# Attention and MLP-mixer on one Trainium2 core: output sums by accumulating DMAs, GpSimd's sums on VectorE, weight sums staged in four places

## The chip, the core and the metric

The kernel runs on one NeuronCore of a Trainium2 chip. TensorE multiplies matrices into PSUM; VectorE, ScalarE and GpSimd do elementwise work; DMAs move data between DRAM and SBUF and are issued from the instruction queues of SyncE (SP), ScalarE or GpSimd. Each engine works its own queue in order. The metric is the device time of one execution in microseconds (us), given as the median of several runs.

## What is computed

```python
kv  = einsum('bhsd,bhse->bhde', k, v)          # 8 batches, 8 heads, 576 tokens, head size 64
out = einsum('bhsd,bhde->bhse', q, kv)
x   = (out / sqrt(mean(out*out, -1) + 1e-6) * g_norm)  # (B,H,S,D) -> x of (B, S, H*D) = (8, 576, 512)
h   = relu(x.transpose(0,2,1) @ w_tok1) @ w_tok2       # token mixing, 576 -> 256 -> 576
u   = x + h.transpose(0,2,1)
out = u + relu(u @ w_ch1) @ w_ch2                      # channel mixing, 512 -> 1536 -> 512
```

All data are 32-bit floats on the chip.

## The kernel before

**First part (to about 197 us).** Attention and token mixing of the eight batches give `u`. Each batch's first 512 tokens are a *unit* in DRAM (`u_dram[0..7]`); the ninth unit holds the last 64 tokens of all batches. Unit 0 is group 0; units 2g-1 and 2g are group g, so groups 1 to 4 have 1024 tokens each.

**Channel mixing by fast multiplication.** Each of the two products with `w_ch1` and `w_ch2` is done by a 2x2 block scheme with seven products instead of eight (Winograd's form of Strassen's), for groups 1 to 4 at two levels: 7 outer times 7 inner products. The scheme needs sums of blocks on every side: sums of the weights, sums of `u` or of the middle result `v`, and sums of the products.

- *Group 0* uses one level: `channel1_once(0)` (TensorE from about 197 us) and `channel2_once(0)` (from 234 us). Beside them run, woven in by `weave`, the sums of the weights for the inner level (`split`): for each weight and outer product o, four sums of 128x384 in a staging tile `sv0`, then DMAs of the seven parts to DRAM (`parts_dram`). In `split`, `first` also sends three unchanged parts; `first` and `second` add on VectorE, `third` and `fourth` on GpSimd; `fourth` issues the DMAs of the four sums. For weight 1 the staging pool has two buffers, for weight 2 one (`svb`, L1292). All these DMAs are issued on SP. `channel2_once` runs its products in the order first, sixth, second, seventh, fifth, fourth, third; product `fourth` adds into the PSUM tile that `seventh` filled, after VectorE has read it there (`u3`, L781), and `third` likewise into that of `fifth`.
- *Groups 1 to 4* run `channel1(g)` and `channel2(g)`. Time is counted in *places*: one inner product is one place, 49 places a stage, and the dictionaries `products` and `beside` say which product and which other steps stand at a place. The program order of every engine is the order of places, kept by `keep_in_program_order`. Channel1 of group g begins at place 98(g-1), its channel2 49 places later, and the next group's channel1 follows without a break. A `put(b + place, ...)` in channel2 with a place above 48 therefore lies in the next group's channel1, and a negative place lies in the stage before.

**One outer product** (`outer`, L816). Its seven inner products use three PSUM names: `a` and `b` with one buffer, `d` with two. Product 1 fills `a`, ScalarE copies it to `d`; product 5 fills `b` and is read as `p5`; product 6 adds into `d`, which is read as `u2`; then products 2, 3, 7 and 4, at the places 0, 1, 3, 4, 5, 6 and 9 of the outer product (`PLACE`, L809). Between a product and the next one that needs its bank back there are at least two places, in which the eviction has to be done. VectorE does the two joins of each outer product, and all six evictions where a base is added (in channel1 for o = 2, 5, 4); otherwise ScalarE copies.

**Other steps in the places.** `inner_u` and `outer_u`: sums of blocks of `u` for the inner and outer level. `inner` (`ins`): sums of `v` for the inner level of channel2, tile `sv`. `add`, `sum1` to `sum4`, `make_a21`: outer sums of `v`. `rectify`: relu by ScalarE. In channel1, outer sum 1 of `v` (four 128x768) and outer sum 7 (two 128x1536) are on GpSimd (L955, L957). `turn_blocks`: VectorE transposes of the next group's units (one `xt` buffer, fetched from `u_dram` by `fetch_t`), whose blocks go to DRAM and come back as `uT` by `fetch_u`. `fetch_w`: the weight parts from `parts_dram`, asked for 4 to 12 places before the first place of their outer product, with two buffers each.

**The output.** An outer product of channel2 leaves a tile [128, 4, 256] in the pools `us` or `r` (three buffers each). `us` also holds the outer sums 5, 6 and 4 of `u`. `xg` holds the group's `u` (fetched by `fetch_x`); nine `xadd` steps of 128x1024 on VectorE add the tiles onto it, one `radd` adds product 6 to product 7, and `store` writes `xg` to the output. Seven of the nine stand at places 45 to 60 of channel2.

Of the kernel before, what the change touches and what calls it, by code (L numbers as in the profile page):

```python
# [20 lines left out]
def kernel(  # L21
# [255 lines left out]

    def split(weight, o):

        at = []  # L280
        wide = lambda t: t if weight == 1 else t.rearrange("p (w e) -> p w e", w=W)
        to = parts_dram[weight, o]

        def of(n):
            if weight == 1:
                return (w_ch1[:, SA[o]] if SA[o] < 4 else late["w2"][:, SA[o] - 4])[:, SA[n]]
            return w2_of(o)[:, ts(int(n in (2, 3)), W), ts(int(n in (7, 3)), P)]

        own = lambda n: wide(at[0][:, OWN[weight][n]])

        def first():
            at.append(late["sv0"].tile([P, 4, FQ], F32, name="sv0"))
            for n in (1, 2, 4 if weight == 1 else 3):
                dma(wide(to[:, POS[n]]), of(n))
            if weight == 1:
                tensor_add(own(5), of(7), of(4))
            else:
                tensor_add(own(5), of(7), of(1), ALU.subtract)

        def second():  # L300
            tensor_add(own(6), own(5), of(1), ALU.subtract) if weight == 1 else tensor_add(
                own(6), of(3), own(5), ALU.subtract)

        def third():
            tensor_add(own(7), of(1 if weight == 1 else 3), of(7), ALU.subtract, nc.gpsimd)

        def fourth():
            tensor_add(own(3 if weight == 1 else 4), of(2), own(6), ALU.subtract, nc.gpsimd)
            t = at[0]
            if weight == 1:  # L310
                dma(to[:, 1:].rearrange("p (g k) f -> p g k f", k=3)[:, :, :2],
                    t.rearrange("p (g k) f -> p g k f", k=2))
            else:
                dma(to[:, 1:3], t[:, :2])
                dma(to[:, 5:], t[:, 2:])

        return [first, second, third, fourth]


# [598 lines left out]
    def channel1(g, n0):  # L918
# [19 lines left out]
        for i, o in enumerate(ORDER1):  # L938
            first(i, o)
            for place, step in zip((-4, -2, 2, 5), inner_u(g, o)):  # L940
# [11 lines left out]
        for place, step in zip((15, 18), add(3, 3, 1)):  # L952
            put(b + place, step)
        for place, i, j in ((27, 0, 0), (29, 0, 1), (30, 1, 1), (32, 1, 0)):
            put(b + place, do(lambda i, j: tensor_add(*(sub(v_tile(g, t), i, j) for t in (1, 4, 3)),  # L955
                                                      engine=nc.gpsimd), i, j))
        for place, step in zip((36, 39), add(7, 5, 4, nc.gpsimd)):  # L957
            put(b + place, step)

        for t, *places in ((2, None, 24, 28, 26), (7, 46, 46, 48, 48), (1, None, 44, 47, 45)):  # L960
# [4 lines left out]
        for k, place in enumerate((12, 17, 23, 27, 33, 37, 42, 46)):  # L965
# [4 lines left out]
        put(b + 70, do(fetch_t, units(g + 2)[0], 0))  # L970
        for place, step in zip((-2, 1, 10, 18), outer_u(g)):
# [3 lines left out]
    def channel2(g, n0):  # L975
# [86 lines left out]
        for place, steps in (  # L1062
                (-12, [ins[1][0]]), (-11, [ins[1][2]]), (-10, [ins[1][1]]), (-8, [ins[1][3]]),
                (3, [ins[2][0]]), (5, [ins[2][1]]), (6, [ins[4][0]]), (7, [ins[2][2]]),
                (8, [A[0]]), (9, [A[1]]), (10, [ins[2][3]]), (11, [S3[0]]), (12, [S3[1]]),
                (13, [ins[4][1]]), (14, [ins[4][2]]), (15, [S2[0]]), (16, [ins[4][3]]), (17, [ins[7][0]]), (18, [xadd(0, 0, 1)]),
                (19, [ins[7][1]]), (21, [S2[1], ins[7][2]]), (23, [ins[7][3]]), (24, [S1[0]]),
                (25, [ins[6][0]]), (26, [S4[0]]), (27, [ins[6][1]]), (28, [S1[1]]), (29, [ins[6][2]]),
                (31, [ins[5][0], ins[6][3]]), (33, [ins[5][1]]), (34, [xadd(0, 0, 2)]),
# [4 lines left out]
        if g < NG - 1:  # L1074
            for place, steps in ((45, [xadd(0, 1, 6)]), (48, [radd(7, 6)]), (50, [xadd(1, 0, 4)]),
                                 (52, [xadd(1, 1, 5)]), (54, [xadd(1, 0, 7)]), (56, [xadd(1, 1, 7)]),
                                 (56, [do(store, g, 1)]), (58, [xadd(0, 1, 5)]),
                                 (60, [xadd(0, 1, 3)]), (60, [do(store, g, 0)]),
                                 (74, [do(fetch_x, g + 1, 0)]), (84, [do(fetch_x, g + 1, 1)])):
                put(b + place, *steps)  # L1080
# [8 lines left out]
        for k in range(4):  # L1089
            put(b + 6 + 2 * k, do(fetch_u, g + 1, k // 2, k % 2))  # L1090
# [201 lines left out]
    late["sv0"] = pool("svb", 1, "right", w2s)  # L1292
    fill, turns = lasts + parts2[:20], turn_unit(2)
    for i, f in enumerate(turns):
        fill.insert(3 * i, f)
    fill.insert(1, do(fetch_u, 1, 0, 0))
    fill.insert(4, do(fetch_u, 1, 0, 1))
    for k in range(4):
        fill.insert(8 + 4 * k, do(fetch_w, 0, k))
    fill.insert(24, do(fetch_w, 1, 0))  # L1300
    fill += [do(fetch_u, 1, 1, 0), do(fetch_u, 1, 1, 1), do(fetch_w, 1, 1)] + inner_u(1, 1)[:2] + outer_u(1)[:1]
    weave(channel2_once(0), fill)
# [12 lines left out]
    for n, f in enumerate(parts2[20:]):  # L1315
        put(2 + 3 * n // 2, f)
    put(2, do(fetch_t, units(2)[0], 0))
    put(16, turn_over)
    put(22, do(fetch_x, 1, 0))
    put(26, do(fetch_x, 1, 1))  # L1320
# [43 lines left out]
```

## Time and profile before

| | |
|---|---|
| median of 7 runs | 869.25 us (867.01 to 871.2) |
| the profiled execution | 870.09 us |
| its span, first to last instruction | 868.3 us |
| mean granted TensorE clock | 0.975 of full speed |
| PE busy | 795.6 us (92%) |
| DVE busy | 641.8 us (74%) |
| ACT busy | 265.1 us (31%) |
| POOL busy | 118.4 us (14%) |
| moved by DMA | 197.36 MB |

Engines are named as in the profile: PE is TensorE's matmul, PEld its weight load, DVE VectorE, ACT ScalarE, POOL GpSimd, SP SyncE (SPq and POOLq are the queues on which DMAs are issued). A line of a timeline gives start and duration in us, the engine, the line of the kernel, the operation, the tile written and the tiles read, partitions x elements, how often it is merged, and in brackets the idle time before it with what ended it. Since helpers record most operations, L122 stands for every elementwise sum and L131 for every matmul: the names of the tiles tell them apart. A line of waits gives the total in us, the number of times and the longest. A line of DMA issues gives the number, the KB of each, and the median us from issue to landing.

### The profile page before, as it was taken

To read this page: it belongs to the slowest core of one execution; us is meant where nothing else is said; L and a number is where in the kernel's file an instruction comes from. 1 tells how busy PE (TensorE), PEld (TensorE's weight loads), DVE (VectorE), ACT (ScalarE), POOL (GpSimd) and SP (SyncE) were. 2 spreads that over 40 slices of the span, in tenths; PEclk is the share of its full clock that TensorE was granted. 3 is DMA by queue.
4 is the path that set the end of the run, shared out by engine and by line. 5 is a ranking of instruction groups with operands and counts; after the bars stand their busy time and mean duration, and the time that the engine had idled before them with its cause. 6 is when DMAs were issued, how large, how long until landed. Compare 5 with 4: busy or idle time off the path is not lost.

```text
span 868.3 us, 14846 instructions
## 1 busy us (share of the span) xinstructions
PE 795.6 (92%) x5832; PEld 658.5 (76%) x5832; DVE 641.8 (74%) x890; ACT 265.1 (31%) x513; POOL 118.4 (14%) x97
## 2 busy tenths in 40 slices
PE   6999999999995698899998799999889999979995
PEld 5655545448884576799987699997779998769995
DVE  3667575986744497878688969778887868895985
ACT  2366565741100122421143052123242113305210
POOL 1302010102413205100002400000510000240000
PEclk9999999999998799999999999999999999999997
DMA  9999993666999987685467867448678546655542
GB/s 296 312 336 340 344 381 131 220 195 208 352 289 298 314 271 241 182 264 157 136 232 239 252 210 233 132 143 292 210 238 276 141 143 221 216 157 140 144 134 73
DMA packets 124773, 197.36 MB, mean 227 GB/s; under 512 B 9376, under 2 KB 75424, under 8 KB 124704
## 3 DMA queue, kind: packets, MB, share of 16 engines
q1 hardware_dynamic: 120400, 185.24, 68.3%
q0 software_dynamic: 2624, 9.44, 2.8%
q10 hardware_dynamic: 1680, 1.74, 0.7%
q8 instruction: 46, 0.75, 0.4%
q14 instruction: 23, 0.19, 0.1%
HBM read 148.80 MB, written 47.58 MB: 226 GB/s over the span
## 4 chain that ended last, share of the span: by engine, by line
PE 50%; DVE 15%; DMA 7%; issue 2%; SPq 2%; POOL 1%; ACT 0%; DVEq 0%; POOLq 0%; ACTq 0%
PE ps_d L131 22%; PE ps_b L131 14%; PE ps_a L131 13%; DVE v L122 4%; DVE sv L122 4%; DMA xt<-u_dram 3%; SPq L119 2%; DVE ui L122 2%; DMA parts<-sv 2%; DVE y L590 1%; DVE u L122 1%; DVE xg L122 1%; POOL sv L122 1%; PE ps_u L131 1%; DMA w<-parts 1%
## 5 line engine op out<-in xcount | busy, mean ns | idle before, releaser
L131 PE MATMUL ps_d<-ui,w 128*128 128x256 f32 x504 | 127.4, 399 | 26.4 <-DVE v L122 13.3
L131 PEld LDWEIGHTS ps_d<-ui,w 128*128 128x128 f32 x504 | 98.0, 199 | 46.9 <-DVE v L122 18.4
L122 POOL TENSOR_TENSOR v<-v,v 128x768 f32<-128x768 f32 (+1 forms) x24 | 57.7, 2409 | 410.6 <-ACT v L128 376.8
L128 ACT COPY ps_d<-ps_a 128x768 f32<-128x768 f32 (+1 forms) x56 | 32.0, 571 | 223.0 <-PE ps_a L131 223.0
L131 PE MATMUL ps_b<-w,sv 128*128 128x128 f32 x672 | 84.9, 276 | 3.9 <-DVE sv L122 3.9
L131 PE MATMUL ps_a<-w,v 128*128 128x128 f32 x672 | 84.2, 275 | 0.0
L131 PEld LDWEIGHTS ps_b<-w,sv 128*128 128x128 f32 x672 | 79.5, 192 | 4.8 <-DVE sv L122 4.7
L131 PEld LDWEIGHTS ps_a<-w,v 128*128 128x128 f32 x672 | 79.8, 192 | 0.2
L122 DVE TENSOR_TENSOR v<-v,v 128x1536 f32<-128x1536 f32 (+1 forms) x46 | 74.4, 1624 | 0.3
L125 ACT ACTIVATE v<-v 128x768 f32<-128x768 f32 (+1 forms) x54 | 42.6, 821 | 95.7 <-DVE v L122 93.4
L131 PE MATMUL ps_d<-w,v 128*128 128x128 f32 x528 | 67.0, 277 | 2.7 <-DVE xg L122 2.7
L131 PE MATMUL ps_u<-h,w_tok 128*128 128x512 f32 (+1 forms) x160 | 67.5, 607 | 0.4 <-ACT ps_u L128 0.2
L131 PEld LDWEIGHTS ps_d<-w,v 128*128 128x128 f32 x528 | 63.4, 194 | 3.0 <-DVE xg L122 2.9
L131 PE MATMUL ps_h<-x,w_tok 128*128 128x512 f32 (+1 forms) x160 | 65.5, 603 | 0.1
L131 PE MATMUL ps_d<-w,sv 128*128 128x128 f32 x480 | 60.1, 275 | 0.0
L131 PE MATMUL ps_b<-ui,w 128*128 128x256 f32 x168 | 42.8, 392 | 18.3 <-DVE ui L122 12.1
L131 PEld LDWEIGHTS ps_d<-w,sv 128*128 128x128 f32 x480 | 57.1, 192 | 0.2
L131 PEld LDWEIGHTS ps_b<-ui,w 128*128 128x128 f32 x168 | 32.3, 195 | 25.2 <-DVE ui L122 12.5
L131 PE MATMUL ps_a<-uT,w 128*128 128x256 f32 x192 | 50.1, 400 | 0.7 <-DVE v L122 0.5
L131 PEld LDWEIGHTS ps_h<-x,w_tok 128*128 128x128 f32 (+1 forms) x160 | 26.1, 189 | 32.1 <-issue 27.7
L131 PEld LDWEIGHTS ps_u<-h,w_tok 128*128 128x128 f32 (+1 forms) x160 | 24.7, 179 | 31.5 <-issue 25.4
L122 DVE TENSOR_TENSOR sv<-v 128x768 f32<-128x768 f32 x40 | 48.6, 1222 | 0.0
(141 smaller groups left out, 1250.9 us busy)
## 6 DMA issues: line engine op xcount, KB each, us to landing
w<-parts SPq DMA_DIRECT2D x168, 384.0 KB, 3.6
w<-parts SPq DMA_DIRECT2D x56, 192.0 KB, 3.1
qT<-in_q_dram SPq DMA_DIRECT2D x8, 1152.0 KB, 9.3
xt<-u_dram SPq DMA_DIRECT2D x36, 256.0 KB, 4.3
blocks<-y SPq DMA_DIRECT2D x72, 128.0 KB, 2.5
uT<-blocks SPq DMA_DIRECT2D x36, 256.0 KB, 4.7
xg<-u_dram SPq DMA_DIRECT2D x9, 1024.0 KB, 6.4
k_in<-in_k_dram SPq DMA_DIRECT2D x16, 512.0 KB, 9.3
```

The costliest lines, as they stand in the source:

```text
L119: keep(engine.dma_start(o, i))
L122: keep(engine.tensor_tensor(out=o, in0=a, in1=b, op=op))
L125: keep(nc.scalar.activation(o, a, AF.Relu))
L128: keep(nc.scalar.copy(o, a))
L131: keep(nc.tensor.matmul(*a, **kw))
L590: keep(nc.vector.transpose(blocks[u][:, :, o, n:n + 2].rearrange("p b n t -> p n b t"), xt[u, i][:, ts(o, DH)].rearrange("p (n b t) -> p n ...
```

## The change

- In `split`, weight 2's staging is no longer one buffer: four places are used in turn, in halves of the tiles v3 and v2 of group 1. All its sums are on VectorE, its DMAs are issued on ScalarE's queue, and the DMAs of a staged split are issued when the next split's fourth sum has been issued. Weight 1 is as before.
- The fill of `channel2_once(0)` is written out anew: all 28 steps of weight 2's sums, the transposes of unit 2, the loads of `uT`, the four inner sums and two outer sums of `u` for group 1 lie in it. Before, eight of the steps and the rest of the `u` sums lay beside channel1 of group 1. `turn_over` moves from place 16 to 9.
- In channel1, GpSimd's six sums go to VectorE, at other places; `inner_u`, `outer_u` and `rectify` get other places; of the eight `turn_blocks`, four lie in channel1 and four in channel2 (places 49 to 80).
- In channel2, the sums of the first outer product stand at -3 to 2 and no longer at -12 to -8; S4 moves from 26 to 29. For groups 1 to 3 `xg` is not fetched: two DMAs copy `u` from DRAM to the output, and nine DMAs on GpSimd's queue add the tiles onto it (`accum_op=ALU.add`); `radd` stays. Group 4 keeps `xg` and `xadd`.

```diff
+        queue, other = (nc.sync, nc.gpsimd) if weight == 1 else (nc.scalar, nc.vector)
...
         def first():
-            at.append(late["sv0"].tile([P, 4, FQ], F32, name="sv0"))
+            if weight == 1:
+                at.append(late["sv0"].tile([P, 4, FQ], F32, name="sv0"))
+            else:
+                n = len(staged)
+                flat = v_tile(1, 3 - n // 2 % 2).rearrange("p s j t -> p (s j t)")
+                at.append(flat[:, ts(n % 2, 4 * FQ)].rearrange("p (k f) -> p k f", k=4))
...
+        def fourth():
+            tensor_add(own(3 if weight == 1 else 4), of(2), own(6), ALU.subtract, other)
+            if weight == 1:
+                put_away()
+            else:
+                staged.append(put_away)
+                if len(staged) > 1:
+                    staged[-2]()
...
-            for place, step in zip((-4, -2, 2, 5), inner_u(g, o)):
+            for place, step in zip((-8, -7, -6, -5) if i == 0 else (-5, -4, 0, 2), inner_u(g, o)):
...
-        for place, step in zip((15, 18), add(3, 3, 1)):
+        for place, step in zip((17, 22), add(3, 3, 1)):
             put(b + place, step)
-        for place, i, j in ((27, 0, 0), (29, 0, 1), (30, 1, 1), (32, 1, 0)):
-            put(b + place, do(lambda i, j: tensor_add(*(sub(v_tile(g, t), i, j) for t in (1, 4, 3)),
-                                                      engine=nc.gpsimd), i, j))
-        for place, step in zip((36, 39), add(7, 5, 4, nc.gpsimd)):
+        for place, i, j in ((27, 0, 0), (32, 1, 1), (34, 0, 1), (41, 1, 0)):
+            put(b + place, do(lambda i, j: tensor_add(*(sub(v_tile(g, t), i, j) for t in (1, 4, 3))), i, j))
+        for place, step in zip((42, 44), add(7, 5, 4)):
             put(b + place, step)
-        for t, *places in ((2, None, 24, 28, 26), (7, 46, 46, 48, 48), (1, None, 44, 47, 45)):
+        for t, *places in ((2, None, 24, 28, 26), (7, 45, 46, 47, 48), (1, None, 44, 47, 46)):
...
-        for k, place in enumerate((12, 17, 23, 27, 33, 37, 42, 46)):
+        for k, place in enumerate((2, 5, 9, 12, 49, 52, 76, 80)):
...
-        put(b + 70, do(fetch_t, units(g + 2)[0], 0))
-        for place, step in zip((-2, 1, 10, 18), outer_u(g)):
+        put(b + 84, do(fetch_t, units(g + 2)[0], 0))
+        for place, step in zip((-2, 1, -1, 10), outer_u(g)):
...
-                (-12, [ins[1][0]]), (-11, [ins[1][2]]), (-10, [ins[1][1]]), (-8, [ins[1][3]]),
+                (-3, [ins[1][0]]), (-1, [ins[1][1]]), (1, [ins[1][3]]), (2, [ins[1][2]]),
...
-                (25, [ins[6][0]]), (26, [S4[0]]), (27, [ins[6][1]]), (28, [S1[1]]), (29, [ins[6][2]]),
+                (25, [ins[6][0]]), (29, [S4[0]]), (27, [ins[6][1]]), (28, [S1[1]]), (30, [ins[6][2]]),
...
         if g < NG - 1:
-            for place, steps in ((45, [xadd(0, 1, 6)]), (48, [radd(7, 6)]), (50, [xadd(1, 0, 4)]),
-                                 (52, [xadd(1, 1, 5)]), (54, [xadd(1, 0, 7)]), (56, [xadd(1, 1, 7)]),
-                                 (56, [do(store, g, 1)]), (58, [xadd(0, 1, 5)]),
-                                 (60, [xadd(0, 1, 3)]), (60, [do(store, g, 0)]),
-                                 (74, [do(fetch_x, g + 1, 0)]), (84, [do(fetch_x, g + 1, 1)])):
-                put(b + place, *steps)
+            def join(i, j, o):
+                u = units(g)[i]
+                return lambda: keep(nc.gpsimd.dma_start(
+                    out[u, :LO, ts(j, DH)].rearrange("(t p) e -> p t e", p=P), rs[o][0], accum_op=ALU.add))
+            for i in range(2):
+                put(b - 6 + 3 * i, do(lambda i: dma(out[units(g)[i], :LO], u_dram[units(g)[i]]), i))
+            for place, step in ((12, join(0, 0, 1)), (20, join(0, 0, 2)), (26, join(1, 0, 4)), (40, join(0, 1, 6)),
+                                (41, radd(7, 6)), (43, join(1, 0, 7)), (44, join(1, 1, 7)), (47, join(0, 1, 5)),
+                                (50, join(1, 1, 5)), (54, join(0, 1, 3))):
+                put(b + place, step)
+            if g == NG - 2:
+                put(b + 60, do(fetch_x, g + 1, 0))
+                put(b + 70, do(fetch_x, g + 1, 1))
...
-        for k in range(4):
-            put(b + 6 + 2 * k, do(fetch_u, g + 1, k // 2, k % 2))
+        for k, place in enumerate((6, 8, 12, 36)):
+            put(b + place, do(fetch_u, g + 1, k // 2, k % 2))
...
+    turns = turn_unit(2)
+    waits = [[do(fetch_u, 1, 0, h) for h in range(2)]] + [[f] for f in lasts[:2]] + [turns[:1]] + [[f] for f in lasts[2:]]
+    for i in range(J):
+        waits += [turns[2 * i + 1:2 * i + 3]] + [[f] for f in parts2[2 * i:2 * i + 2]]
+        if i < 2:
+            waits += [[do(fetch_w, 0, 2 * i), do(fetch_w, 0, 2 * i + 1)]]
+    waits += [[f] for f in parts2[8:16]] + [[do(fetch_u, 1, 1, 0), do(fetch_w, 1, 0)]]
+    waits += [[f] for f in inner_u(1, 1)] + [[do(fetch_u, 1, 1, 1), do(fetch_w, 1, 1)]]
+    waits += [[f] for f in parts2[16:]] + [[do(fetch_t, units(2)[0], 0)]] + [[f] for f in outer_u(1)[:1]]
+    waits += [[lambda: staged[-1]()], outer_u(1)[2:3]]
+    weave(channel2_once(0), [do(lambda fs: [f() for f in fs], fs) for fs in waits])
```

## The prediction

> **What bounds it now.** I read the stretches of the span first, then TensorE's waits, then the timelines of VectorE, GpSimd and TensorE side by side, then the DMA list. The stretches (columns: stretch, length, busy us of PE, PEld, DVE, ACT, POOL with counts, granted clock, DMA share, GB/s):
>
> ```profile
> 271.60:299.50 27.90, 11.68 (x37) 9.11 (x37) 10.99 (x17) 3.18 (x4) 6.84 (x6) 0.70 0.92 300
> 433.00:508.00 75.00, 67.44 (x304) 56.74 (x303) 64.54 (x86) 24.74 (x33) 14.42 (x6) 0.98 0.72 227
> 508.00:574.60 66.60, 65.62 (x581) 65.27 (x581) 49.48 (x58) 13.75 (x34) 0.00 (x0) 1.00 0.65 193
> ```
>
> The last row is a channel2: TensorE is full. The middle row is a channel1: VectorE is busy 64.5 of 75 us and TensorE is not full. The first row is the start of group 1: TensorE mostly idle, on a low clock. A product of channel1 takes 1.295 us when it is not held up (starts 1.29 to 1.30 us apart in TensorE's timeline), of channel2 1.340, so 49 places are worth 63.5 and 65.7 us. By the first product of each stage the four channel1 took 94.3, 74.8, 74.4 and 73.0 us, the first three channel2 66.9 each. Above the full rate that is 30.8, 11.3, 10.9, 9.5 and 1.2 each. Of the 30.8, 18.8 lie in the first seven places (271.65 to 299.52 for 9.07 us) and 12.0 in the rest.
>
> ```profile
> PE ps_d L131 <- DVE v L122: 13.3, 8, 2.6
> PE ps_b L131 <- DVE ui L122: 12.1, 1, 12.1
> PE ps_d L131 <- DVE u L122: 9.1, 4, 2.5
> PE ps_b L131 <- DVE v L122: 6.2, 5, 1.7
> PE ps_b L131 <- DVE sv L122: 3.9, 4, 1.0
> ```
>
> TensorE waits for VectorE alone; the 12.1 is the start of group 1, the rest recurs four times. Why VectorE is late, from its timeline and then GpSimd's:
>
> ```profile
> 604.84 0.75 DVE L122 TENSOR_TENSOR ui<-uT,ui 128x256 f32<-128x256 f32 x2
> ...
> 623.10 3.98 DVE L122 TENSOR_TENSOR ui<-us,ui 128x256 f32<-128x256 f32 x2
> ...
> 632.15 3.50 DVE L122 TENSOR_TENSOR sv<-v 128x768 f32<-128x768 f32 x1
> ```
>
> ```profile
> 623.32 3.48 POOL L122 TENSOR_TENSOR v<-v,v 128x1536 f32<-128x1536 f32 x1 [2.30 <-DVE v L122]
> ...
> 631.30 3.54 POOL L122 TENSOR_TENSOR v<-v,v 128x1536 f32<-128x1536 f32 x1 [4.50 <-DVE v L122]
> ```
>
> Two small sums that take 0.75 us take 3.98 while GpSimd adds; a 0.95 us sum takes 3.50. TensorE stops 2.59 and 2.47 us behind them:
>
> ```profile
> 628.66 2.86 PE L131 MATMUL ps_d<-ui,w 128*128 128x256 f32 x12 [2.59 <-DVE v L122]
> ...
> 636.58 1.98 PE L131 MATMUL ps_d<-ui,w 128*128 128x256 f32 x6 [2.47 <-DVE u L122]
> ```
>
> **VectorE in channel1, by parts.** Start to start, its steps cost 0.87 us (128x768), 0.335 (256), 1.14 (1024), 1.67 (1536), 0.68 (a pair of transposes). Seven places give it 9.07 us. Before, by the places in the code, the seven outer products ask for 7.6, 8.3, 10.9, 5.3, 9.1, 16.5 and 4.6 us. The third: five evictions 4.35, four inner sums of u 1.34, two halves of v3 3.34, transposes 0.68, an outer sum of u 1.14. The sixth: six evictions 5.22, inner 1.34, transposes 0.68, four sv sums 3.48, and 5.8 lost behind GpSimd (3.98 less 0.75, 3.50 less 0.95). Exactly these two overrun and are followed by the stalls.
>
> The edits: *outer sums to DMAs* take seven xg sums of 1.14 (8.0 us) out of the first two outer products of groups 2 to 4, and two more from channel2. *GpSimd's six sums to VectorE* cost four of 0.87 and two of 1.67, 6.8 us; the six excesses in VectorE's timeline (0.50, 1.61, 0.32, 0.34, 3.2, 2.55) give back 8.5. *Half of the transposes* go to channel2 (2.7 us); the sv sums of the next stage go from place 37-41 to 46-51; the last outer sum of u from 18 to 10. After, the seven sums are 4.9, 5.6, 7.4, 6.5, 7.4, 7.4 and 8.4 us, 47.6 of 63.5, none above 9.07. In the third, the eviction that frees bank a ends 0.1 place before it is needed. Channel2 gains 2.7 of transposes and loses 2.3 of xg sums: no change, under 66 us of products. S4's half moves from 26 to 29, out from between the two sums that TensorE waits 0.98 for: 1.0 per channel2, 4 groups.
>
> *New waits in VectorE's queue.* Transposes now stand at 2, 5, 9, 12 and their one xt buffer is fetched behind each; xt lands 3.5 us (2.7 places) after issue in this stage, 2.6 to 5.4. Chained with the block stores (1.8 us of SP's queue), the transpose of place 12 ends near place 15.5; behind it the eviction that the product at place 16 needs ends near 16.2: 0.4 us. At the least nothing, at 5.4 us some 2. With the tight bank of the third I take 1.2 us a group. So channel1 of groups 2 to 4 gains 31.7 - 3.6 = 28.1, the rest of group 1 12.0 - 1.2 = 10.8, channel2 4.0.
>
> **The adding DMAs.** No row shows one. Nearest are the same queue's plain stores:
>
> ```profile
> u_dram<-x POOLq DMA_DIRECT2D x16, 512.0 KB, 5.1
> ```
>
> The same 512 KB, 0.7 us of GpSimd each, 5.1 us to land. The Trainium skill (DMA: Bandwidth & Descriptors, Anatomy of one DMA) fits 2.0 us plus bytes over 436 GB/s, an estimate of 3.2; the row, taken in busy DMA, decides. An addition also reads its destination, so up to twice: 5.1 to 10.2; I take 7. Below 5.1 is not expected: it moves no less. The same page (Rules for kernel authors) speaks against the change: nothing guards the bytes between an accumulate's read and write, so the next access must wait for the earlier DMA's semaphore. Were the DMAs free of each other, the last join would be issued at place 52 of channel2 and land near 57. Under the rule it also waits for the join of o=5, that for o=6 (place 40). At X = 7 us (5.4 places) that is 40, 45.4, then 52 for its own data, landing near 58, with 0.7 us of descriptors. Who needs it: the outer sum of u at place 59 takes that us buffer, and VectorE's evictions stand behind it. So 0 us at 7 with the wait or without it; at 12 us the chain ends at 67.6 and TensorE loses some 7 us in each of three groups. GpSimd has nothing else queued there. Bytes: each of three groups drops 2 MB of xg loads and 2 MB of stores, adds 2 MB of copies and 4.5 MB of joins (9 if counted twice): 8 to 23 us of DMA time at the 298 GB/s that a full share gives, on 97 of 141. Weights are fetched 12 places (15 us) ahead and land in 4.9: hidden. The copies are issued at -6 and -3 on SP, 18 places ahead of the first join: hidden.
>
> **The start of group 1.** In channel2_once the program order on VectorE decides. Before:
>
> ```profile
> 245.59 0.77 DVE L590 STREAM_TRANSPOSE y<-xt 128x256 f32<-128x256 f32 x2 [2.40 <-DMA xt<-u_dram]
> ...
> 259.97 0.56 DVE L122 TENSOR_TENSOR sv<-w_ch 128x384 f32<-128x384 f32 x1 [7.22 <-DMA parts<-sv]
> 260.45 0.68 DVE L122 TENSOR_TENSOR us<-ps_c,us 128x512 f32<-128x512 f32 x1
> ```
>
> ```profile
> 261.19 5.45 PE L131 MATMUL ps_c<-d,v 128*128 128x256 f32 x24 [1.09 <-DVE us L122]
> ```
>
> The one staging buffer costs 7.22 here, and 24.1 in all, and pushes u's inner sums to 284. Four places take that away. But now all four transposes of unit 2 stand ahead of that us eviction, with one xt buffer between them, and in this stretch xt lands after
>
> ```profile
> xt<-u_dram SPq DMA_DIRECT2D x4, 256.0 KB, 5.1
> ```
>
> The first fetch now follows four uT loads (ended 244.9): landed 250.0, transposed 250.7; the next lands 255.9, then 2.2 us of block stores on SP, then about 263.5 and 268.6 (4.5 and 4.3, as fewer weights move). Three weight sums of 0.48 and the eviction follow: 271.5. The fourth product, due at 259.95, starts at 271.6: 11.6 us in place of 1.09. With 2.2 us of low clock, as after the 12.1 us stop, and 5.2 us each, channel2_once ends at 284.2. The rest of the weight sums fit in VectorE until 286.8; the store that follows them on ACT's queue holds the copy of bank a: 0.6 us at place 3. Place 7 comes at 293.9, not 299.5: 5.6 gained. With hops of 2.6 us it is some 16, with 6.7 it is -2.
>
> **Sum.** 868.3 - 28.1 - 10.8 - 4.0 - 5.6 = 819.8 us of span; 1.8 lie around it (870.09 against 868.3) and the median is 0.8 below the profiled run: 821 us.
>
> **Rivals.** (1) The start of group 1 opens as well: fast hops, 16 gained instead of 5.6: 810, and 805 with no rest in channel1. For it: less weight traffic on SP; against: 0.93 DMA share there. (2) The joins land in 9 to 14 us because the DMA engines are full in channel2 (0.65 now, 0.95 or more with joins counted twice and blocks moved in): VectorE stops at place 59; at 12 us 821 + 21 = 842. (3) Slower: the same wait when X passes about 15 us. The chain 40 + 3X then ends near 75 (place 26 of channel1), 16 us lost in each of three groups, which eats the 48; at 18 us it ends near 82, about 25 each: 895. Against it: a plain store needs a third of that. (4) The change doesn't reach TensorE: what VectorE gives up is returned by waits for xt and us, 869.
>
> **Chances.** My forecast 0.55 (812 to 830), (1) 0.17, (2) 0.19, (3) 0.07, (4) 0.02. A measurement of this kernel tells about 0.2% from no change. Range 805 to 846: it leaves out (3), (4), the tip of (1) and the upper half of (2). Faster 0.91, same 0.02, slower 0.07.
>
> **What would show it.** Right: no GpSimd sums beside channel1, no 3.5 us sums on VectorE, channel1 of groups 2 to 4 within 66 us, channel2 within 66; a stop of some 10 us in the last products of channel2_once, with y<-xt as VectorE's wait. Wrong: VectorE waiting at the us sum for a DMA to the output (rival 2 or 3); TensorE waiting for w<-parts; the fourth product of channel2_once on time (rival 1).

## The result, and the profile after

The changed kernel takes 862.03 us (median of 12 runs, 856.73 to 865.44) against 869.42 for the kernel before beside it: a ratio of 0.991, 95% interval 0.9893 to 0.9926. It is faster, but by 7 us and not by the 48 predicted, and 862 lies outside the range of 805 to 846. The profiled execution is the quickest of the twelve, 856.73 us with a span of 854.9, so 5.3 us of the distance between 821 and 862 lie between this profile and the median; the lines below explain 35.1 us, 819.8 to 854.9.

The same stretches as before, by their place in the program: the first seven places of group 1 and a little behind them, channel1 of group 2, channel2 of group 2 (stretch, length, busy us of PE, PEld, DVE, ACT, POOL with counts, granted clock, DMA share, GB/s; a share can come out slightly above 1):

```profile
284.10:308.20 24.10, 13.90 (x57) 11.66 (x56) 10.79 (x18) 4.68 (x6) 0.00 (x0) 0.79 0.93 330
429.20:500.10 70.90, 65.99 (x302) 57.02 (x301) 49.57 (x71) 24.41 (x33) 2.54 (x2) 0.98 0.81 226
500.10:568.10 68.00, 65.93 (x583) 65.57 (x582) 53.92 (x69) 14.06 (x35) 8.96 (x7) 1.00 0.93 242
```

VectorE has been relieved as meant: 49.6 busy us in channel1 where it had 64.5. But TensorE is still not full there, 66.0 of 70.9, and channel2, which was full, now loses 2 us. DMA shares rose from 0.72 to 0.81 and from 0.65 to 0.93. What TensorE waits for now, and two of VectorE's waits:

```profile
PE ps_c L131 <- DVE us L122: 11.3, 1, 11.3
PE ps_d L131 <- ACT ps_d L128: 10.2, 1, 10.2
PE ps_b L131 <- DVE v L122: 9.7, 3, 3.4
PE ps_b L131 <- DVE sv L122: 7.6, 4, 2.1
...
PE ps_d L131 <- DVE v L122: 3.0, 4, 1.4
```

```profile
DVE y L606 <- DMA xt<-u_dram: 52.2, 18, 7.3
...
DVE us L122 <- DMA out_dram<-us: 6.7, 1, 6.7
```

The stops behind stretched sums are gone (the 13.3 us behind `v` have become 3.0). In their place VectorE itself waits for an output DMA and for the single `xt` buffer, 52.2 us, where before it was

```profile
DVE y L590 <- DMA xt<-u_dram: 10.7, 8, 2.4
```

In channel1 of group 2 this reads so, VectorE first, then TensorE:

```profile
450.81 0.77 DVE L606 STREAM_TRANSPOSE y<-xt 128x256 f32<-128x256 f32 x2 [6.32 <-DMA xt<-u_dram]
451.50 0.38 DVE L122 TENSOR_TENSOR ui<-uT,ui 128x256 f32<-128x256 f32 x1
451.80 1.22 DVE L122 TENSOR_TENSOR us<-uT,us 128x1024 f32<-128x1024 f32 x1
452.94 0.95 DVE L122 TENSOR_TENSOR v<-ps_b,u 128x768 f32<-128x768 f32 x1
```

```profile
449.04 1.46 PE L131 MATMUL ps_a<-uT,w 128*128 128x256 f32 x6
453.94 2.67 PE L131 MATMUL ps_b<-ui,w 128*128 128x256 f32 x6 [3.45 <-DVE v L122]
```

A transpose that nobody needs soon stands at the head of VectorE's queue and waits for its data; three steps behind it is the eviction that frees bank b. This `xt` was issued at 443.54 on SP and landed 7.1 us later, not 3.5. The stop costs its 3.45 us and more, since the six matmuls behind it take 2.67 us where they take 1.46 at full clock. In group 4, which has no transposes beside it, the same eviction is late behind the other wait:

```profile
725.80 1.23 DVE L122 TENSOR_TENSOR us<-uT,us 128x1024 f32<-128x1024 f32 x1 [6.73 <-DMA out_dram<-us]
726.94 0.95 DVE L122 TENSOR_TENSOR v<-ps_b,u 128x768 f32<-128x768 f32 x1
```

The chain of adding DMAs behind it, on GpSimd:

```profile
698.75 3.87 POOL L1092 DMA_DIRECT2D out_dram<-r  x3 [5.88 <-issue]
711.12 1.27 POOL L1092 DMA_DIRECT2D out_dram<-r  x1 [8.49 <-DMA out_dram<-r]
716.05 1.29 POOL L1092 DMA_DIRECT2D out_dram<-us  x1 [3.66 <-DMA out_dram<-r]
```

The last addition could be issued only when the earlier one to the same bytes had landed, at 716.05, place 57.5 of channel2 where 52 was predicted; it landed 9.7 us later, at place 65 and not 58. The queue of these DMAs, and their issues (KB each, median us to landing):

```profile
q0 software_dynamic: 16880, 23.60, 14.1%
...
out_dram<-r POOLq DMA_DIRECT2D x15, 512.0 KB, 9.1
...
out_dram<-us POOLq DMA_DIRECT2D x12, 512.0 KB, 8.2
```

Before, that queue had 2624 packets, 9.44 MB and 2.8%. So 27 additions of 0.524 MB bring 14256 packets, 528 each, and 14.1% of 854.9 x 16 less 2.8% of 868.3 x 16, or 1540 engine-us: 57 each, 3.6 us of all sixteen engines.

### The profile page after: what moved, and what is told of

Same layout as the page of the kernel before. It is cut to its first block, busy times and chain, and to the rows that moved or that the text cites. A ratio compares the mean times of both kernels' runs of the same rounds, so it can differ in the third digit from the quotient of the medians.

```text
span 854.9 us, 14847 instructions
## 1 busy us (share of the span) xinstructions
PE 791.6 (93%) x5832; PEld 660.6 (77%) x5832; DVE 610.0 (71%) x901; ACT 264.9 (31%) x513; POOL 79.1 (9%) x86
## 3 DMA queue, kind: packets, MB, share of 16 engines
q1 hardware_dynamic: 103840, 169.31, 62.5%
q0 software_dynamic: 16880, 23.60, 14.1%
## 4 chain that ended last, share of the span: by engine, by line
PE 47%; DMA 15%; DVE 10%; issue 3%; SPq 1%; POOL 1%; ACT 1%; DVEq 0%; ACTq 0%; POOLq 0%
PE ps_d L131 20%; PE ps_b L131 13%; PE ps_a L131 12%; DMA xt<-u_dram 7%; DVE v L122 3%; DMA out_dram<-r 2%; DVE sv L122 2%; DVE y L606 1%; DMA w<-parts 1%; DMA uT<-blocks 1%; SPq L119 1%; DMA out_dram<-us 1%; DVE us L122 1%; DMA parts<-w_ch 1%; PE ps_u L131 1%
## 5 line engine op out<-in xcount | busy, mean ns | idle before, releaser
L131 PE MATMUL ps_d<-ui,w 128*128 128x256 f32 x504 | 122.8, 389 | 13.2 <-ACT ps_d L128 10.2
L122 DVE TENSOR_TENSOR v<-v,v 128x1536 f32<-128x1536 f32 (+2 forms) x70 | 103.0, 1477 | 0.3
L131 PEld LDWEIGHTS ps_a<-w,v 128*128 128x128 f32 x672 | 79.8, 192 | 0.2
L131 PEld LDWEIGHTS ps_d<-w,v 128*128 128x128 f32 x528 | 63.9, 195 | 3.0 <-DVE xg L122 2.9
L606 DVE STREAM_TRANSPOSE y<-xt 128x256 f32<-128x256 f32 x72 | 27.6, 422 | 53.1 <-DMA xt<-u_dram 52.2
L1092 POOL DMA_DIRECT2D out_dram<-us x12 | 15.4, 1279 | 383.6 <-ACT us L128 278.2
L131 PE MATMUL ps_a<-uT,w 128*128 128x256 f32 x192 | 47.5, 383 | 0.4
L432 DVE TENSOR_TENSOR x<-ps_o,g_sb 128x512 f32<-128x512 f32 x32 | 21.5, 687 | 34.1 <-PE ps_o L131 29.4
```

Of the source, the lines that this page charges most:

```text
L122: keep(engine.tensor_tensor(out=o, in0=a, in1=b, op=op))
L131: keep(nc.tensor.matmul(*a, **kw))
L432: keep(nc.vector.tensor_mul(x, bank[c, h], g_sb.to_broadcast([P, number(c), D])))
L606: keep(nc.vector.transpose(blocks[u][:, :, o, n:n + 2].rearrange("p b n t -> p n b t"), xt[u, i][:, ts(o, DH)].rearrange("p (n b t) -> p n ...
L1092: return lambda: keep(nc.gpsimd.dma_start(out[u, :LO, ts(j, DH)].rearrange("(t p) e -> p t e", p=P), rs[o][0], accum_op=ALU.add))
```

## The experiments

Times are medians; the bracket is the ratio to the kernel before, with its 95% interval. Stage lengths are from first product to first product, as in the prediction.

**Weight DMAs on SP (e1).** The parts of weight 2 go back to SP's queue.

```diff
-        queue, other = (nc.sync, nc.gpsimd) if weight == 1 else (nc.scalar, nc.vector)
+        queue, other = (nc.sync, nc.gpsimd) if weight == 1 else (nc.sync, nc.vector)
```

> The changed kernel, with weight 2's part DMAs issued on SP again and no longer on ScalarE's queue. Theory (ScalarE's copy of bank a is held behind the last part DMAs on its queue): TensorE's 10.2 us wait for ACT ps_d at place 3 of group 1 goes to under 1 us, and the time falls by about 10 us to 852. Rival (the DMA engines themselves are full there, the queue is only where it shows): the same 8 to 10 us reappear in that place as a wait for uT, w or u sums behind a later SP queue, and the time stays within 3 us of 862. The 11 us stop of the fourth product in channel2_once should stay in both, or grow, since SP then carries the block stores, xt and the parts.

863.96 us (0.9932, 0.9904 to 0.9959): nothing gained. ScalarE's stop of 10.2 us is gone, and TensorE stops 12.4 us five places later (place 8, not 3), behind VectorE, which now waits for `xt` behind the parts in SP's queue; channel2 of group 1 begins at 363.3, where it began at 359.4:

```profile
289.14 0.42 DVE L122 TENSOR_TENSOR ui<-us 128x256 f32<-128x256 f32 x1
301.19 0.77 DVE L606 STREAM_TRANSPOSE y<-xt 128x256 f32<-128x256 f32 x2 [11.62 <-DMA xt<-u_dram]
```

**Two xt buffers (e2).** Each transpose's rows are fetched one transpose earlier.

```diff
-                put(b + place + 1, do(fetch_t, units(g + 1)[(k + 1) // J], (k + 1) % J))
+                put(b + place + 1, do(fetch_t, units(g + 1)[(k + 2) // J], (k + 2) % J))
...
-    late["xt"] = pool("xt", 1)
+    late["xt"] = pool("xt", 2)
...
```

> The changed kernel with two xt buffers for groups 1 to 4 and unit 2, each fetched one transpose earlier. Theory (VectorE stands in program order behind single-buffered xt loads): the 52 us that VectorE waits for xt fall below 20, the 11.3 us stop of channel2_once's fourth product falls to 2 to 6, and channel1 of groups 2 and 3 loses its stops (1.4 and 3.5, 0.8 and 2.9); but the us sum at place 59 must still wait for the join of o=3, so only 1 to 2 us of each may go. Total 862 to 850. Rival (the loads are slow because the joins fill the DMA engines, an earlier issue only moves the queue): xt waits stay above 35 us and the time within 3 us of 862.

862.04 us (0.9917, 0.9899 to 0.9936): nothing again, although VectorE's waits for `xt` fell from 52.2 to 23.6 us. The time went to the other wait, once in each of three groups:

```profile
DVE y L606 <- DMA xt<-u_dram: 23.6, 5, 8.1
DVE us L122 <- DMA out_dram<-us: 18.1, 3, 10.7
```

**The output summed by VectorE (e3).** `xg`, the `xadd` steps and the store return, with the last two sums at places 57 and 58; the rest of the change stays.

```diff
-                return lambda: keep(nc.gpsimd.dma_start(
-                    out[u, :LO, ts(j, DH)].rearrange("(t p) e -> p t e", p=P), rs[o][0], accum_op=ALU.add))
...
+            for place, steps in ((45, [xadd(0, 1, 6)]), (48, [radd(7, 6)]), (50, [xadd(1, 0, 4)]),
+                                 (52, [xadd(1, 1, 5)]), (54, [xadd(1, 0, 7)]), (56, [xadd(1, 1, 7)]),
+                                 (56, [do(store, g, 1)]), (57, [xadd(0, 1, 5)]),
+                                 (58, [xadd(0, 1, 3)]), (60, [do(store, g, 0)]),
...
```

> The changed kernel with the output summed by VectorE into xg again, as before (the last two sums at places 57 and 58, as the us buffer must be free at 59), no joins and no copies. Theory (joins cost more through xt and us than VectorE's sums would): xt lands in 3.5 to 4 us again, not 7, the wait for a DMA to the output is gone, channel1 of groups 2 to 4 takes 66 to 69 us in place of 70.9, 68.9, 70.5, and the time falls by 3 to 9 us. Rival (VectorE's load was the binding cost, and the joins pay): channel1 of groups 2 to 4 takes 71 us or more, since the first two outer products again ask for 8.3 and 9.0 of 9.07 us, and the time rises by 3 us or more.

854.86 us (0.9833, 0.9804 to 0.9862). Channel1 of group 4 takes 63.9 us, the full rate; groups 2 and 3 take 69.9 and 70.3, with one stop of 3.7 to 3.9 us, still behind `xt`. So doing the additions by DMA was not only no gain: it cost some 7 us against the work it replaced.

**Plain stores instead of additions (e5).** The same DMAs write without adding. This leaves out most of the output's sums.

```diff
-                    out[u, :LO, ts(j, DH)].rearrange("(t p) e -> p t e", p=P), rs[o][0], accum_op=ALU.add))
+                    out[u, :LO, ts(j, DH)].rearrange("(t p) e -> p t e", p=P), rs[o][0]))
```

> The changed kernel with the joins as plain stores: the same bytes on the same queue, but they overwrite and don't add, so most of the output's sums are left out. Theory (the addition itself costs DMA time): a join lands in 5 to 6 us, not 8 to 9, the software queue's share falls from 14% to some 6%, xt lands sooner, and the time falls by 4 to 8 us. Rival (descriptors of 1 KB, or the number of DMAs, are the cost): landing stays at 8 us or more and the time within 2 us of 862.

843.25 us (0.9692, 0.9663 to 0.9721): 19 us less than with the addition. Channel1 of groups 2 to 4 takes 66.3, 64.4 and 63.9, and VectorE waits for no output DMA.

```profile
q0 software_dynamic: 6512, 23.60, 7.5%
...
out_dram<-r POOLq DMA_DIRECT2D x15, 512.0 KB, 5.4
...
out_dram<-us POOLq DMA_DIRECT2D x12, 512.0 KB, 5.8
```

The same bytes in 144 packets each instead of 528, and 7.5% of 844.3 x 16 less the 389 engine-us of the rest: 23 engine-us each. The addition takes 2.5 times the engine time of the store, and lands 2.4 to 3.7 us later.

**GpSimd's sums on VectorE, alone (e4).** The kernel before, with its six sums in channel1 moved at their old places.

```diff
-            put(b + place, do(lambda i, j: tensor_add(*(sub(v_tile(g, t), i, j) for t in (1, 4, 3)),
-                                                      engine=nc.gpsimd), i, j))
+            put(b + place, do(lambda i, j: tensor_add(*(sub(v_tile(g, t), i, j) for t in (1, 4, 3))), i, j))
-        for place, step in zip((36, 39), add(7, 5, 4, nc.gpsimd)):
+        for place, step in zip((36, 39), add(7, 5, 4)):
```

> The kernel before, with one part of the change alone: GpSimd's six sums in channel1 (four of 128x768, two of 128x1536) done by VectorE at their old places. My theory: they cost VectorE 6.8 us and give back 8.5 us of stretched sums, so the sixth outer product still asks more than its 9.07 us, but less than before: channel1 of groups 2 to 4 falls from 74.8, 74.4, 73.0 to 71 to 73, no sum of 128x256 takes over 1 us, 858 to 866 us in all (4 to 12 below the kernel before). Rival (GpSimd's sums were free cover, and the gain came only from the outer sums that left VectorE): channel1 grows by up to 6.8 us a group, 875 to 895 us.

855.57 us (0.9826, 0.9805 to 0.9848): this one edit to the kernel before gains twice what the whole change does. Channel1 took 91.5, 71.4, 70.8 and 68.9 us, 2.9 to 4.2 less in every group, and the stretch of group 2 reads:

```profile
430.50:501.90 71.40, 65.35 (x302) 55.54 (x302) 62.51 (x91) 24.41 (x33) 0.00 (x0) 1.00 0.76 239
```

With six more sums VectorE is busy 62.5 us in this stage, where it was 64.5: the sums cost less than they had stretched the others.

**Three splits later (e7).** The last 12 of the 28 weight-2 steps stand beside channel1 of group 1, with a staging buffer of their own and their DMAs on SP.

```diff
+                if n >= 4:
+                    at.append(late["sv0"].tile([P, 4, FQ], F32, name="sv0"))
...
-    waits += [[f] for f in parts2[16:]] + [[do(fetch_t, units(2)[0], 0)]] + [[f] for f in outer_u(1)[:1]]
+    waits += [[f] for f in parts2[16:16]] + [[do(fetch_t, units(2)[0], 0)]] + [[f] for f in outer_u(1)[:1]]
...
-    put(9, turn_over)
+    for n, f in enumerate(parts2[16:]):
+        put(3 + 3 * n // 2, f)
+    put(22, turn_over)
...
```

> The kernel after, with the last three weight-2 splits (12 of the 28 steps) moved back beside channel1 of group 1, through one staging buffer and with their DMAs on SP. Theory (the 10.2 us stop in the first places of group 1 is ScalarE's copy of bank a, standing in its queue behind DMAs of weight parts that are issued at 1.2 us each because the DMA engines are full): the stop goes below 2 us, channel1 of group 1 falls from 75.3 to about 68, 852 to 857 us. Rival (the transition is filled by the bytes, wherever they are issued): the stop moves to VectorE or to the weights of the second outer product, channel1 of group 1 stays at 73 to 76, 860 to 864 us.

861.54 us (0.9895, 0.9854 to 0.9936): no gain. The stop behind ScalarE is gone and group 1 begins 4.7 us earlier, at 279.5; but its channel1 takes 79.8 us, and channel2 starts at 359.28 where it started at 359.44. My theory of this run was wrong; its rival was right in the time, and in that the stop moved (to 4.3 us at place 7 and 3.4 behind VectorE).

**Channel2 in another order (e8).** The last inner sum of product 6 ahead of what it was queued behind: the first sum of product 5, S4 and the last pair of transposes. In this order `S4` reads half of a tile after a sum of product 6 has overwritten a block of it, so a part of the operand of product 3 is another value.

```diff
-        for k, place in enumerate((2, 5, 9, 12, 49, 52, 76, 80)):
+        for k, place in enumerate((2, 5, 9, 12, 49, 52, 76, 82)):
...
-                (25, [ins[6][0]]), (29, [S4[0]]), (27, [ins[6][1]]), (28, [S1[1]]), (30, [ins[6][2]]),
-                (31, [ins[5][0], ins[6][3]]), (33, [ins[5][1]]),
+                (25, [ins[6][0]]), (32, [S4[0]]), (27, [ins[6][1]]), (28, [S1[1]]), (29, [ins[6][2]]),
+                (30, [ins[6][3]]), (31, [ins[5][0]]), (33, [ins[5][1]]),
```

> The kernel after, with four steps of channel2 in another order: sums 2 and 3 of outer product 6 at places 29 and 30, the first of product 5 at 31, S4 behind them at 32, and the last pair of transposes at 82 instead of 80. Theory (the stop of 2.06 us at place 33 of channel2 is VectorE working through S4, transposes and an inner sum of product 5 before the inner sum that product 33 reads): the stop falls under 0.5 us, channel2 of groups 1 to 3 from 69.8, 68.0, 68.0 to 67.8, 66.2, 66.2, 6 to 8 us less in all, 854 to 856. Rival (VectorE is late here because of what is queued before place 29, so the order of these four does not matter): the stop stays near 2 us or appears at places 34 to 36, 860 to 863 us.

854.61 us (0.9822, 0.9803 to 0.9841). The stop is gone and channel2 of groups 1 to 3 takes 65.65 each, down from 69.8, 68.0 and 68.0. Of these 8.8 us, channel1 gave some back: that of group 3 grew from 68.9 to 71.7, and that of group 4 from 70.5 to 73.5, behind VectorE's wait of 11.0 us for an output DMA.

**All four at once (e9).** e3, e2, e7 (the staging in the memory of group 0's `xg`) and e8's order together, so that a part of the operand of product 3 is another value here too.

> All undone that the runs so far blame: the output summed on VectorE as in the kernel before (last sums at 57 and 58), two xt buffers fetched one ahead, three weight-2 splits beside channel1 of group 1 with their DMAs on SP, and the order of channel2's four steps as in the run that changes it alone. Theory (each of the four costs is separate): the terms add, 7 from the additions, 8 from group 1, 6 to 8 from channel2, some 4 from xt, less 2 lost to the later sums: 836 to 842 us, channel1 of groups 2 to 4 at 64 to 66. Rival (they share one cause, so that one cure takes the gain of the next): no better than the sum on VectorE alone, 850 to 855 us.

824.72 us (0.9479, 0.9462 to 0.9495). Channel1 of groups 2 to 4 takes 63.86 us each, channel2 of groups 1 to 3 65.79: TensorE's full rate in six stages. The sum exceeds its terms: against the changed kernel e3, e2, e7 and e8 alone gave 7, 0, 0 and 7 us, and together they give 37. So the terms aren't separate costs that add: each alone is in part covered by the others.

**VectorE's sum and two xt buffers (e10).** e3 with e2.

> The kernel with the output summed on VectorE (as in the run that did this alone, 854.9 us) and two xt buffers fetched one ahead. Theory (without the additions the only stop left in channel1 of groups 2 and 3, 3.7 to 3.9 us at place 12, is the wait for one xt buffer): channel1 of groups 2 and 3 falls from 69.9 and 70.3 to 64 to 66, 843 to 848 us. Rival (place 12 is late because the outer sums of the output took VectorE's time there): both stay at 69 to 70, 853 to 856 us.

838.49 us (0.9635, 0.9603 to 0.9667): 16 less than e3, where 7 to 12 were expected, with channel1 of groups 2 and 3 at 63.86. Two buffers are worth nothing beside the additions' waits, and 16 us without them.

**The additions with room (e13).** The additions stay, `xt` has two buffers, and the tile of outer product 3 lies, in groups 1 to 3, in the memory of `xg`, which is empty there.

```diff
-                    r[0] = late[name].tile([P, J, DH], F32, name=name, tag=name)
+                    if o == 3:
+                        r[0] = late["xg"].tile([P, J, DM], F32, name="xg")[:, :, :DH]
+                    else:
+                        r[0] = late[name].tile([P, J, DH], F32, name=name, tag=name)
...
```

> The additions kept, and both waits that were seen behind them taken away: two xt buffers fetched one ahead, and for groups 1 to 3 the output of outer product 3 in the memory of xg, which stands empty there, so that no sum of u waits for the join of product 3. Theory (the additions cost through these two waits alone): VectorE waits for no output DMA, channel1 of groups 2 to 4 at 64 to 66, 844 to 850 us. Rival (the additions cost DMA engine time, and what is late next takes the place: inner transfers, weights, uT): channel1 of groups 2 to 4 stays at 68 to 71, 855 to 862 us.

840.64 us (0.9671, 0.9644 to 0.9698), a little below the theory's band: channel1 of groups 2 to 4 takes 65.2, 68.4 and 63.9, and no step of VectorE waits for an output DMA. The additions still land as late as before:

```profile
out_dram<-r POOLq DMA_DIRECT2D x15, 512.0 KB, 9.8
...
out_dram<-us POOLq DMA_DIRECT2D x9, 512.0 KB, 8.6
```

So it is not their landing that costs, but who stands behind it: the sum that needs their tile, and the `xt` loads that are late beside them.

**The room alone (e14).** e13's tile, one `xt` buffer.

> The kernel after, with the output of outer product 3 in the memory of xg, one xt buffer as it was. Theory (the waits for xt and for the join of product 3 stand one behind the other in VectorE's queue, and either alone gives the late time to the other): channel1 of groups 2 and 3 stays at 68 to 70, that of group 4 (no transposes beside it) falls to 64 to 66, 853 to 858 us. Rival (the wait for the join is the one that decides): 842 to 848 us, channel1 of groups 2 and 3 at 64 to 66 too.

853.25 us (0.9812, 0.9774 to 0.9851): group 4 falls to 63.9, groups 2 and 3 stay at 70.9 and 71.3 behind `xt`. The two waits stand one behind the other, and in groups 2 and 3 either alone keeps the time: two buffers 0, room 9, both 21. And e14 shows how much of the addition's cost goes through `xt`: e5 has one `xt` buffer too and no wait for an output DMA either, and with plain stores its channel1 of groups 2 and 3 takes 66.3 and 64.4, and the whole 10 us less.

**All four, S4 in its old place (e12).** As e9, with `S4` at 26 and the last two sums of product 6 at 29 and 30; every part of the output is computed.

```diff
-                (25, [ins[6][0]]), (29, [S4[0]]), (27, [ins[6][1]]), (28, [S1[1]]), (30, [ins[6][2]]),
-                (31, [ins[5][0], ins[6][3]]), (33, [ins[5][1]]),
+                (25, [ins[6][0]]), (26, [S4[0]]), (27, [ins[6][1]]), (28, [S1[1]]), (29, [ins[6][2]]),
+                (30, [ins[6][3]]), (31, [ins[5][0]]), (33, [ins[5][1]]),
```

> As the run that undoes all four costs, with another order of channel2's steps: S4 at 26 as in the kernel before, sums 2 and 3 of outer product 6 at 29 and 30, the first of product 5 at 31, the last transposes at 82. Theory (place 33 is on time whenever the last sum of product 6 stands ahead of the first of product 5 and of the transposes): channel2 stays at 65.8, 824 to 827 us. Rival (it is S4 between the sums, wherever it stands before place 30): a stop of 1 us in each channel2, 829 to 832 us.

824.93 us (0.9487, 0.9464 to 0.9509), the best complete version, 44 us below the kernel before. Its channel1 and channel2 of group 2:

```profile
421.90:485.80 63.90, 63.81 (x302) 56.03 (x302) 57.16 (x78) 24.45 (x33) 0.00 (x0) 1.00 0.77 250
485.80:551.50 65.70, 65.70 (x583) 65.54 (x582) 55.55 (x71) 14.06 (x35) 0.00 (x0) 1.00 0.72 212
```

TensorE is busy all the time in both stages, as it was in neither the kernel before nor the one after, and VectorE does the output's sums beside it.

**All cures, with the additions (e15).** e12 with e13's additions in place of VectorE's sums.

> The additions kept, and everything cured that was found: two xt buffers, room for the last tile, three weight-2 splits beside channel1 of group 1, and channel2 in the order of the run with S4 at 26. Theory (the additions cost nothing by themselves once nobody waits for them, and the sums that they take from VectorE were not needed at full rate either): within 3 us of the same kernel with the sum on VectorE, 822 to 828 us. Rival (the additions fill the DMA engines, so that the transposes and the inner transfers are late whatever waits are removed): channel1 of groups 2 and 3 at 66 to 69, 829 to 836 us.

828.55 us (0.9538, 0.9515 to 0.956), at the edge of the two bands. Channel1 of groups 2 and 3 takes 65.1 and 65.2, 1.3 above the full rate, with stops of 0.8 and 0.9 us. The additions, once nobody waits for them, cost about 4 us against VectorE's sums and gain nothing: at full rate VectorE had room for them.

## Why the prediction was wrong, step by step

The steps against the profiles, in us of span gained:

| step | predicted | after | all cured, e12 |
|---|---|---|---|
| up to the start of group 1's channel2 (predicted: 5.6 and 10.8) | 16.4 | 6.52 | 9.73 |
| channel1 of groups 2 to 4 | 28.1 | 11.94 | 30.65 |
| channel2 of groups 1 to 3, then group 4's and the end | 4.0 | -5.06 | 4.86 |
| sum | 48.5 | 13.40 | 45.24 |

Of the 35.1 us that are missing, 16.2 lie in channel1 of groups 2 to 4, 9.9 in the start of group 1 and its channel1, and 9.1 in channel2 and the end.

- **VectorE's ledger held, but it was not what decided.** It put VectorE's work in channel1 at 47.6 us, and 49.6 were measured; with 57 us, and the output's sums among them, e10 and e12 still run at 63.86 us a stage. So these sums need not have left VectorE. What failed is the remainder of 1.2 us a group above the full rate of 63.5: it was 7.4, 5.4 and 7.0. The part on GpSimd's sums held: predicted 8.5 given back for 6.8, 1.7 net, measured 2.0 less busy time in e4; what it is worth alone, 14 us over the four channel1, I had not worked out.
- **The step that failed first: "At X = 7 us ... landing near 58 ... 0 us at 7 with the wait or without it".** The size was wrong (9.1 and 8.2 us in the median, up to 15.0 in the last channel2 of the three), and with it the place: 65 and not 58, past the sum of `u` at 59. The mechanism was rival 2's. The chain is as long as it is because the kernel keeps the rule that the prediction took from the Trainium skill (DMA: Bandwidth & Descriptors, Rules for kernel authors: wait for the earlier accumulate's semaphore): GpSimd's wait for `out_dram<-r` is 37.8 us in six. No run here shows what would come of not waiting. I priced the addition up to twice a store in landing time; in engine time it is 2.5 stores, which e5 shows. The sum of the bytes was not wrong: 8 to 23 us more of DMA time were predicted, and channel1 and channel2 of group 2 have 121 of 139 us where it was 97 of 141, 23 more. What failed is "hidden": at a DMA share of 0.93 in channel2, and of 1.15 at the start of channel1, the other transfers came late.
- **The second: "xt lands 3.5 us (2.7 places) after issue in this stage" and the 0.4 us that followed from it.** In channel1 of group 2 the first two fetches landed after 7.0 and 7.1 us, above even the 5.4 of the range. The 3.5 came from a stage without additions, and the last additions of a group fall on just the places where `xt` is now fetched. The first 15 us of this stage without additions (e3), with plain stores (e5) and with the additions (columns as above; the second last is the DMA share):

```profile
432.00:447.00 15.00, 15.00 (x78) 13.37 (x78) 14.93 (x20) 6.34 (x9) 0.00 (x0) 1.00 0.58 161
430.80:446.00 15.20, 15.20 (x79) 13.55 (x78) 8.16 (x15) 6.57 (x9) 1.50 (x2) 1.00 0.90 285
429.00:444.00 15.00, 13.63 (x71) 11.88 (x70) 7.94 (x14) 5.13 (x7) 2.54 (x2) 1.00 1.15 266
```

  The same two fetches landed after 2.6 and 3.9 us in e3, after 4.7 and 4.1 in e5, and after 7.0 and 7.1 here. But one buffer costs without additions too: e3 loses 6 us in each of groups 2 and 3 at the fourth transpose, whose rows landed 5.7 us after issue. That the two waits cover each other (e2, e14, e13) is why the cure for one showed little or nothing, and why I, having priced each at about nothing, missed them together. Worked out: 65.2 + 68.4 + 63.9 in e13 against 70.9 + 68.9 + 70.5 is 12.8 us for both in the spans.
- **"S4's half moves ..., out from between the two sums that TensorE waits 0.98 for: 1.0 per channel2" was a misreading.** In the kernel before, VectorE had caught up behind S4: it stood idle for 0.54 us, waiting for TensorE, shortly before the sum in question, so S4's old place cost nothing. Place 33 waits for the last sum of product 6, and the new order puts more ahead of it:

```profile
542.83 0.96 DVE L122 TENSOR_TENSOR v<-v 128x768 f32<-128x768 f32 x1
543.71 0.42 DVE L122 TENSOR_TENSOR u<-ps_d,us 128x256 f32<-128x256 f32 x1
544.04 0.76 DVE L606 STREAM_TRANSPOSE y<-xt 128x256 f32<-128x256 f32 x2
544.72 0.92 DVE L122 TENSOR_TENSOR sv<-v 128x768 f32<-128x768 f32 x1
545.56 0.95 DVE L122 TENSOR_TENSOR sv<-v,sv 128x768 f32<-128x768 f32 x1
```

```profile
546.56 1.60 PE L131 MATMUL ps_b<-w,sv 128*128 128x128 f32 x12 [2.07 <-DVE sv L122]
```

  VectorE's last line is the sum, at 545.56. The transposes of 544.04 are one of the pairs that I had booked as free in channel2, the first sum of product 5 stands behind them, and S4, now at 29, ends just before these lines. TensorE's stop of 0.98 became 2.07: the sign of this step was wrong. With the sum ahead of both transposes and product 5 (e8; e12, with `S4` back at 26) channel2 takes 65.7, which is worth 8.6 us between after and e12 (205.75 less 197.13 for three stages). The three moves were not tried one by one.
- **The start of group 1: the stop before it was read rightly (11.6 us; 11.26), with the four transposes behind it. That place 0 came at 284.19 where 284.2 was predicted is in part luck:** the fourth product started 0.8 us early and the two products took 0.8 us longer than summed. **Then "holds the copy of bank a: 0.6 us" failed: 10.2.** ScalarE's queue from the trace:

```profile
286.89 3.87 ACTq L119 DMA_DIRECT2D parts<-w_ch  x3
290.86 5.34 ACTq L119 DMA_DIRECT2D parts<-v  x4
296.30 0.78 ACT L128 COPY ps_d<-ps_a 128x768 f32<-128x768 f32 x1 [56.79 <-DMA parts<-v]
```

  Seven issues take 9.2 us, and the copy that product 6 needs stands behind them. I had counted one store of the tail, not all seven. But e1 and e7 show that the queue is only where it shows: off ScalarE's queue, the time returns at later places, and channel2 begins no earlier (363.3 in e1, 359.3 in e7, 359.4 after). With e7's edit and two `xt` buffers together (e12) it begins at 356.2, so 3 us were a matter of order. For the rest the bytes are the likely limit: the stretch has a DMA share of 0.92 before, 0.93 after and 0.93 in e7, and in the stop itself, 284.1 to 297.0, it is 1.07. No run here took bytes away from it, so the cause stays open.
- **What is left.** With the waits of channel1 and channel2 cured, e12's span is 823.1 and the prediction's 819.8. The 3.3 are the start of group 1 (6.7 short), less what channel1 and channel2 gave above the sum. The rivals: (2) named the right wait and gave 842; 862 lies beyond it because `xt`, channel2's order and the start of group 1 came on top. (4), that waits for `xt` and `us` give back what VectorE gives up, had 0.02; by the mechanism it was the nearest to the truth.

## What to carry to other kernels

When a relieved engine's queue also holds steps that wait for transfers, price those waits at the landing times of the new places and beside the transfers that the change itself adds, not at those of the old places, and treat them as one chain: if each of two covers the other, taking one away may show nothing. A transfer that adds is paid in DMA engine time and in order (the next access of the same bytes waits), so give its source a buffer that nobody needs back soon, or let an engine with room do the sum. And before a large rearrangement is judged, its smallest part should be run alone: here six sums moved from GpSimd to VectorE gave twice the gain of the whole.

## What the runs showed of the hardware

- An adding DMA of 512 KB took 528 packets and 57 engine-us where a plain one to the same addresses took 144 and 23; landing 8.2 to 9.1 us against 5.4 to 5.8.
- An `xt` fetch of 256 KB landed after 2.6 us where the DMA share of the stretch was 0.58, after 4.7 us at 0.90, and after 7.0 us beside additions at 1.15.
- Seven DMA issues took 9.2 us of ScalarE's queue while the DMA share was 1.07, about 1.3 each, and its compute instruction stood behind them.
- Two stops of the same length in channel2, of groups 1 and 2, did not cost the same:

```profile
406.05 2.59 PE L131 MATMUL ps_b<-w,sv 128*128 128x128 f32 x12 [2.06 <-DVE sv L122]
...
546.56 1.60 PE L131 MATMUL ps_b<-w,sv 128*128 128x128 f32 x12 [2.07 <-DVE sv L122]
```

  Behind the first the granted clock was 0.66 for 5 us, 1.7 us more; behind the second it stayed at 1.00. That is how group 1's channel2 came to 69.8 us where groups 2 and 3 took 68.0. A short stop can so cost nearly twice its length.
